# Float16 attention products, constant scales and a range flag in a fused attention and MLP kernel

## The chip, the cores and the metric

The kernel runs on one core of a Trainium2 chip. The metric is the device time of one execution in microseconds. Engines are named as in the profile: PE is TensorE (matmuls), PEld its weight loads, DVE is VectorE, ACT is ScalarE, POOL is GpSimd, SP is SyncE, which issues nearly all DMAs.

## The reference

There are 8 batches of 8 heads with 576 tokens and 64 dimensions per head. Each k and q row is projected to 128 features, shifted by its own largest absolute projection, and turned into 256 features by two exponentials. Linear attention follows, then an MLP on 4,608 tokens of width 512 with 2,048 hidden units.

```python
def phi(x):
    proj = np.einsum('bhsd,df->bhsf', x, w_phi)
    proj = proj - np.max(np.abs(proj), axis=-1, keepdims=True)
    return np.concatenate([np.exp(proj), np.exp(-proj)], axis=-1)
...
num = np.einsum('bhsf,bhfd->bhsd', q_p, kv)
den = np.einsum('bhsf,bhf->bhs', q_p, z)[..., None] + 1e-06
...
h = x @ w_in
g = h * (1.0 / (1.0 + np.exp(-1.702 * h)))
return (g @ w_out).astype(np.float32)
```

The two MLP weight matrices arrive as float64, everything else as float32.

## The kernel before, in words

All arithmetic is recorded first and ordered afterwards. `Recorder.record` (L164) notes each operation with its engine, its tiles and an estimated cost; `schedule` (L283) plays the five engines forward in time with these costs and picks, on each engine, the ready operation with the lowest priority number; `emit` (L393) writes the instructions in that order, so every one of them carries line L399 in the profile, and tiles tell them apart. Priorities come from `part(v0, v1)`, which gives a group of operations a place on a scale whose unit is one MLP chunk of 384 tokens. One engine executes its instructions in the order written.

Precision is kept by splitting. A float32 value is held as a high and a low 16-bit part, and a product is made of three 16-bit products (high x high, high x low, low x high). The MLP ("MoE" in the code, `moe_chunk`, L1140) works so: for a chunk of 256 or 384 tokens and each of 16 hidden blocks, 12 matmuls into `hb`, a tanh on ACT (`th`), a product on DVE (`g`), a split into `gh` (ACT) and `gl` (DVE), and three 512-column matmuls per 128 tokens into `ab`.

Attention works on units of one batch and two heads (32 units, `attn_unit`, L922) plus a tail per batch for tokens 512 to 575 (`attn_tail`, L865). The first five units are "exact": transposes, projections and products in float32 (`project_whole`, L790; tiles `e`, `vn`, `kf`, `wb`), with no scale needed. The other 27 scale k and q by powers of two found from their maxima (`kq_scales`, L745), split them (`xs`), transpose them by DMA (`xT`), project with `ph`, subtract the maximum (`t`), and for queries transpose `t` back on PE. Of the two exponentials, exp(t) is split into float16 parts (`eh`, `el`) and exp(-t), whose range is larger, into an fp32r part (`eh`) and a bfloat16 part (`elb`). So of the products with v (`vs`, `v`) and with the key sums (`kzs`, `kz`, `kzb`) half are 16-bit and half have one wide fp32r factor. A key step or query step is four matmuls: two of 132 columns, two of 66.

Scales are computed on the chip. `batch_max` (L645) reads v once more for its maximum; `weight_scales` (L592) finds the largest weights from the diagonal of products of each weight block with itself on PE (the `wsq` matmuls, L563); only then can `split_weights` (L621) split the blocks. The float64 weights are turned into float32 by ACT, POOL and DVE in `load_weights` (L524), with staging room inside the weight buffer and the `x` buffers.

Of the kernel before, what the change touches and what calls it, by code (L numbers as in the profile page):

```python
# [8 lines left out]
F32 = mybir.dt.float32  # L9
# [15 lines left out]
EPS = 1e-6  # L25

# [71 lines left out]
class _Op:  # L98
    __slots__ = (
        "eng", "meth", "args", "kw", "cost", "deps", "left", "outs", "allocs", "uses",  # L100
        "prio", "load", "passes", "end", "est", "also", "start", "calls",
# [4 lines left out]
_SWITCH = 0.0  # L106
# [3 lines left out]
class _Engine:  # L110
# [3 lines left out]
    def __getattr__(self, meth):  # L114
        def f(*a, also=(), **k):
            self.rec.record(self.name, meth, a, k, also)

        return f


class Recorder:
    def __init__(self, nc):
        self.nc, self.ops = nc, []
        self.groups, self.first = [], ()
# [4 lines left out]
    def part(self, v0, v1, first=()):  # L129

        self.group = []
        self.groups.append((v0, v1, first, self.group))
        self.first = first

    def pairs(self, mm, also=()):


        o = _Op()
        o.eng, o.meth, o.args, o.kw, o.calls = "tensor", "matmul", (), {}, mm
        c = [self.cost("tensor", "matmul", a, k) for a, k in mm]  # L140
        o.load, o.cost, o.passes = c[0][0], _SWITCH + sum(x[1] * x[2] for x in c) / 2, 1
        o.deps, o.outs, o.allocs, o.uses = {}, [], [], []
        o.end, o.est = None, 0.0
        for a, _ in mm:
            for i in (1, 2):
                if isinstance(a[i], V):
                    self.touch(o, a[i], False)
        for a, _ in mm:
            self.touch(o, a[0], True)
        for a in also:  # L150
            self.claim(o, a.tl)
        o.left = len(o.deps)
        for d in o.deps:
            d.outs.append(o)
        self.group.append(o)
        o.prio = o.eng in self.first
        self.ops.append(o)
# [6 lines left out]
    def record(self, eng, meth, args, kw, also):  # L164
        o = _Op()
        o.eng, o.meth, o.args, o.kw, o.calls = eng, meth, args, kw, None
        c = self.cost(eng, meth, args, kw)
        o.load, o.cost, o.passes = c if eng == "tensor" else (0.0, c, 1)
        o.deps, o.outs, o.allocs, o.uses = {}, [], [], []
        o.left, o.end, o.est = 0, None, 0.0  # L170
# [13 lines left out]
        o.prio = eng in self.first  # L184
# [28 lines left out]
    @staticmethod  # L213
    def shared(o):

        ap = [a.t if isinstance(a, V) else a for a in o.args]
        src = [a for a in ap[1:] if hasattr(a, "space")]
        if any("PSUM" in str(a.space) for a in src):
            return False
        if o.eng == "gpsimd":  # L220
            return len(src) > 1
        if o.eng == "vector":
            return o.meth in ("tensor_copy", "tensor_scalar") or len(src) > 1
        return False

    @staticmethod
    def cost(eng, meth, args, kw):
# [9 lines left out]
        if eng == "tensor":  # L237
# [10 lines left out]
            return (load, n / 2.4 + (22.0 if wide else 3.0), 1)  # L248
        src = ap[1] if len(ap) > 1 and hasattr(ap[1], "space") else out
        psum = "PSUM" in str(src.space)  # L250
        if eng == "scalar":
            return n / 1.2 + 51 + (0 if psum else 42) + 93 * scalars
# [12 lines left out]
        if meth == "tensor_scalar":  # L265
            return 100 + 3.4 * n
        if meth == "tensor_copy":
            return 100 + 0.9 * n
        if meth in ("tensor_sub", "tensor_mul", "tensor_add", "tensor_tensor"):
            return 100 + 2.2 * n  # L270
        return 400.0

    @staticmethod
    def mode(o, i):

        if o.calls:
            return o.calls
# [5 lines left out]
    def schedule(self):  # L283
# [15 lines left out]
        free = {e: 0.0 for e in ("tensor", "scalar", "vector", "gpsimd", "sync")}  # L299
# [4 lines left out]
        def ready(o):  # L304
            est = 0.0
# [9 lines left out]
            cand[o.eng].append(o)  # L315
# [5 lines left out]
        while todo:  # L321
            best = None
            for e, c in cand.items():
                t = free[e]
                pick = None
                for o in c:
                    s = max(t, o.est, turn + o.load) if e == "tensor" else max(t, o.est)
                    ok = True
                    had = {}
# [14 lines left out]
                    if pick is None or k < pick[0]:  # L344
                        pick = (k, o, s)
# [4 lines left out]
            _, o, s = best  # L350
            if o.eng in ("vector", "gpsimd") and self.shared(o):
                if o.eng == "vector":
                    s = max(s, port)
                else:
                    port = s + o.cost
            cand[o.eng].remove(o)
# [6 lines left out]
            if o.meth.startswith("dma"):  # L363
                free[o.eng] = s + (600.0 if o.eng == "sync" else 800.0)
                pipe = max(pipe, s) + o.cost
                o.end = pipe + 1800.0
# [26 lines left out]
    def emit(self):  # L393
        g = lambda a: a.get() if isinstance(a, V) else a
        self.order = self.schedule()
        for o in self.order:
            f = getattr(getattr(self.nc, o.eng), o.meth)
            for args, kw in o.calls or ((o.args, o.kw),):
                f(*[g(a) for a in args], **{k: g(a) for k, a in kw.items()})  # L399
# [3 lines left out]
def attn_moe_kernel(ctx, tc, q, k, v, w_phi, w_in, w_out, out):  # L403
# [11 lines left out]
    NEX = 5  # L415
    NH = 2

# [10 lines left out]
    def static(name, shape, dt):  # L428
# [6 lines left out]
        kq=2, vn=1, xs=2, xT=2, ks=12, tl=1, t=5, e=3, eh=3, ekth=1, eqth=1, xf=1, kzs=1, kf=1, lq=2, nf=1, nt=1, xo=1, x=3, th=2, g=2, gh=2,  # L435
        gl=2, osb=2, sm=8, rc=2, sc=6,
    )
    shapes = dict(
        kq=([P, 2, 8, D], F32), vn=([P, 8, D + 2], F32), xs=([P, 8, 2, D], F16),
        xT=([P, 8, P], F16), ks=([P, 2], F32), tl=([P, 3, NHP, D], F32), t=([P, 4, NF], F32),  # L440
        e=([P, 1024], F32), eh=([P, 512], F32R), ekth=([P, 512], F32R),
        eqth=([P, 512], F32R),
        xf=([P, 4, 2, D], F32),
        kzs=([P, 2, 2, 2, D + 2], F32R), kf=([P, 2, 2, D + 2], F32), lq=([P, 3, D + 2], F32),
        nf=([P, 8, D + 2], F32), nt=([P, 8, D + 2], F32), xo=([P, 2, 4, P], F16),
        x=([P, 2, NCT, S], F16), th=([P, CH], F32), g=([P, CH], F32),
        gh=([P, CH], F16), gl=([P, CH], F16), osb=([P, DM], F32), sm=([P, 4], F32),
        sc=([P, 10], F32), rc=([P, 8], F32),
    )
    pools = {  # L450
        nm: buf(nm, sh, dt, NB[nm], ordered=nm not in ("sc",)) for nm, (sh, dt) in shapes.items()
    }

    NL = dict(eh=3, el=2, ekth=1, ektl=1, eqth=1, eqtl=1)
    for nm in NL:
        pools[nm + "6"] = buf(nm + "6", [P, 512], F16, NL[nm])
    for nm in ("el", "ektl", "eqtl"):
        pools[nm + "b"] = buf(nm + "b", [P, 512], BF16, NL[nm])

# [5 lines left out]

    def psa():
        return R.tile(at, whole=True)

    def f32(ap):
        return ap.bitcast(F32)  # L470
# [6 lines left out]
    nc.vector.tensor_copy(ii[D:P], ident[D:P, D:P])  # L477

    ones = cp.tile([2, P], F32, name="ones")
    nc.gpsimd.memset(ones, 1.0)  # L480
    wone = cp.tile([2, 2], F32, name="wone")
    nc.vector.tensor_scalar(wone[:, 0:1], ident[0:2, 0:1], 16.0, None, ALU.mult)
    nc.vector.tensor_copy(wone[:, 1:2], ident[0:2, 1:2])
# [4 lines left out]
    phg = static("phg", [P, 1], F32)  # L488
    phs = static("phs", [P, 1], F32)

    def load_phi():
# [8 lines left out]
        allmax(phg, wst)  # L500
        R.vector.tensor_scalar(phg, phg, 2.0**-14, None, ALU.mult)
        R.vector.reciprocal(phs, phg)
# [808 lines left out]
```

## Time and profile before

| | |
|---|---|
| median of 3 runs | 1081.53 us (1080.89 to 1082.6) |
| span of the profiled execution | 1079.0 us |
| what lies around the span, median less span | 2.5 us |
| PE, DVE, ACT, POOL busy | 1046.1, 851.1, 713.4, 247.1 us |
| mean granted TensorE clock | 0.995 |
| first MoE matmul, last MoE matmul (start) | 78.42 us, 1073.02 us |
| DMA | 88.59 MB, mean 82 GB/s |

The profiled execution has no time of its own besides its span; the runs' median stands for it. A row of the profile names engine, operation, output<-inputs, shape, count, then busy time (overlaps counted once) and mean duration of one, then idle time of the engine just before these instructions and what ended it. A matmul's duration includes its way through the pipeline, so the next one can start long before the end. In the timeline, the first column is the start in the span and the second the length of a merged run.

### The profile page before, as it was taken

To read this page: it belongs to the slowest core of one execution; us is meant where nothing else is said; L and a number is where in the kernel's file an instruction comes from. 1 tells how busy PE (TensorE), PEld (TensorE's weight loads), DVE (VectorE), ACT (ScalarE), POOL (GpSimd) and SP (SyncE) were. 2 spreads that over 40 slices of the span, in tenths; PEclk is the share of its full clock that TensorE was granted. 3 is DMA by queue.
4 is the path that set the end of the run, shared out by engine and by line. 5 is a ranking of instruction groups with operands and counts; after the bars stand their busy time and mean duration, and the time that the engine had idled before them with its cause. 6 is when DMAs were issued, how large, how long until landed. Compare 5 with 4: busy or idle time off the path is not lost.

```text
span 1079.0 us, 22925 instructions
## 1 busy us (share of the span) xinstructions
PE 1046.1 (97%) x8943; PEld 723.7 (67%) x8943; DVE 851.1 (79%) x1772; ACT 713.4 (66%) x1488; POOL 247.1 (23%) x320
## 2 busy tenths in 40 slices
PE   5998999999999999999999999999999999999997
PEld 3665677778766666678866666677876666577653
DVE  5879999999999997987899978987889675232323
ACT  4778797777878686875786676866687665332322
POOL 5666113331122213211223113111133112000000
PEclk9998999999999999999999999999999999999999
DMA  8956233434343443331244342432232110000101
GB/s 277 301 186 173 87 88 70 100 76 97 76 97 94 114 98 72 82 89 31 62 126 112 57 84 50 94 84 36 56 73 60 31 40 20 1 31 2 30 1 30
DMA packets 177452, 88.59 MB, mean 82 GB/s; under 512 B 143424, under 2 KB 168128, under 8 KB 177088
## 3 DMA queue, kind: packets, MB, share of 16 engines
q1 hardware_dynamic: 177184, 86.87, 32.5%
q8 instruction: 70, 1.15, 0.4%
q10 hardware_dynamic: 160, 0.26, 0.1%
q14 instruction: 38, 0.31, 0.1%
HBM read 54.59 MB, written 9.44 MB: 59 GB/s over the span
## 4 chain that ended last, share of the span: by engine, by line
PE 76%; DVE 13%; ACT 5%; issue 3%; DMA 1%; SPq 1%; POOL 0%; DVEq 0%; ACTq 0%; POOLq 0%
PE ab L399 30%; PE hb L399 29%; PE at L399 17%; DVE sm L399 2%; DVE wbuf L399 2%; DVE gl L399 1%; DVE t L399 1%; ACT e L399 1%; DVE ks L399 1%; DVE el L399 1%; DVE xs L399 1%; DVE elb L399 1%; DVE g L399 1%; SPq L399 1%; DVE vs L399 1%
## 5 line engine op out<-in xcount | busy, mean ns | idle before, releaser
L399 PE MATMUL hb<-x,wbuf 128*128 128x192 f16 (+3 forms) x3264 | 476.4, 280 | 1.2 <-DVE g L399 0.6
L399 PEld LDWEIGHTS <-wbuf 128*128 128x128 f16 (+1 forms) x3392 | 286.4, 98 | 79.9 <-issue 1.8
L399 PE MATMUL ab<-wbuf,gh 128*128 128x512 f16 x1152 | 337.9, 380 | 0.5 <-ACT gh L399 0.3
L399 ACT ACTIVATE th<-hb,usc 128x384 f32<-128x384 f32 (+1 forms) x208 | 115.8, 558 | 145.5 <-PE hb L399 142.8
L399 PE MATMUL ab<-wbuf,gl 128*128 128x512 f16 x576 | 194.1, 379 | 1.4 <-DVE gl L399 1.1
L399 DVE SCALAR_TENSOR_TENSOR g<-th,hb 128x384 f32<-128x384 f32 (+1 forms) x208 | 107.1, 516 | 95.6 <-ACT th L399 93.3
L399 PEld LDWEIGHTS <-gh 128*128 128x128 f16 x1152 | 107.7, 98 | 81.1 <-ACT gh L399 2.6
L399 ACT ACTIVATE gh<-g,al 128x384 f16<-128x384 f32 (+1 forms) x176 | 106.9, 607 | 52.6 <-DVE g L399 52.0
L399 DVE SCALAR_TENSOR_TENSOR gl<-g,al,gh 128x384 f16<-128x384 f32 (+1 forms) x176 | 109.9, 625 | 39.9 <-ACT gh L399 31.4
L399 POOL TENSOR_TENSOR xf<-nf,rc 128x512 f32<-128x512 f32 x28 | 34.2, 1220 | 410.8 <-DVE rc L399 331.3
L399 PE MATMUL at<-ph,xT 128*128 128x128 f16 x976 | 102.4, 219 | 0.0
L399 DVE TENSOR_REDUCE sm<-at 128x4 f32<-128x512 f32 x126 | 85.6, 680 | 17.8 <-PE at L399 17.4
L399 ACT ACTIVATE e<-at 128x512 f32<-128x512 f32 x144 | 85.4, 601 | 20.8 <-PE at L399 19.7
L399 ACT ACTIVATE e<-t 128x512 f32<-128x512 f32 x144 | 88.2, 630 | 11.8 <-DVE t L399 11.1
L399 DVE SCALAR_TENSOR_TENSOR t<-at,ks,sm 128x512 f32<-128x512 f32 x122 | 90.4, 743 | 1.1
L399 PEld LDWEIGHTS <-gl 128*128 128x128 f16 x576 | 54.8, 98 | 50.4 <-DVE gl L399 8.9
L399 DVE TENSOR_TENSOR el<-e,eh 128x512 f16<-128x512 f32 x108 | 75.4, 698 | 13.3 <-ACT eh L399 11.5
L399 DVE TENSOR_TENSOR elb<-e,eh 128x512 bf16<-128x512 f32 x110 | 77.9, 708 | 5.7 <-ACT eh L399 4.3
L399 PE MATMUL at<-vs,eh 128*128 128x132 f32 x216 | 81.8, 379 | 0.0
L399 PE MATMUL at<-kzs,eh 128*128 128x132 f32 x224 | 79.4, 373 | 0.8 <-ACT nf L399 0.5
L399 PEld LDWEIGHTS <-xT 128*128 128x128 f16 x976 | 69.8, 98 | 12.9 <-issue 0.3
L399 ACT ACTIVATE eh<-t 128x512 fp32r<-128x512 f32 x109 | 67.1, 635 | 1.1 <-DVE t L399 1.1
(199 smaller groups left out, 1845.6 us busy)
## 6 DMA issues: line engine op xcount, KB each, us to landing
vn<-in_v_dram SPq DMA_DIRECT2D x64, 128.0 KB, 2.7
kq<-in_k_dram SPq DMA_DIRECT2D x32, 256.0 KB, 3.2
kq<-in_q_dram SPq DMA_DIRECT2D x32, 256.0 KB, 3.0
tl<-in_v_dram SPq DMA_DIRECT2D x18, 384.0 KB, 3.2
x<-in_moe_w_in_dram SPq DMA_DIRECT2D x10, 512.0 KB, 6.0
x<-in_moe_w_out_dram SPq DMA_DIRECT2D x10, 512.0 KB, 6.3
out_dram<-osb SPq DMA_DIRECT2D x36, 128.0 KB, 2.4
out_dram<-osb SPq DMA_DIRECT2D x16, 256.0 KB, 2.5
```

The costliest lines, as they stand in the source:

```text
L399: f(*[g(a) for a in args], **{k: g(a) for k, a in kw.items()})
```

## The change

**Products.** Every key and query step becomes six matmuls of 66 columns with float16 parts (`keys`, `numden`). exp(-t) is brought into float16 range by a constant factor. For queries, the projection is made a second time with `ph` as stationary and the transposed rows as moving operand (one 512-column pair, `project_q`), so that features come out transposed without a transpose of `t`; the shift by the maximum is not subtracted from queries but put back as a factor per token (`cs`, from ACT) on one half of numerator and denominator (`n1`).

**Exact units.** Batch 0 keeps float32 keys in its four units and float32 queries for the first half of the tokens (`queries_exact`); its other queries, its tail and the fifth unit go in float16 parts. `attention_first` records all keys of batch 0, then the first half of the queries, then the second, after which MLP chunks can start on 256 columns.

**Scales.** All scales are constants (`PH, VS, ONE, WS, GS`). The maxima of k, q and v before use, the self-products of the weights and the second pass over them go. Each weight block is split when it is loaded, in six elementwise operations through three staging buffers (`raw`): one on ACT, two scalings on DVE, ACT or POOL, one on DVE, a copy and a subtraction.

**Range flag.** The maxima of v, of the weights and of w_phi, a ratio of sums (`art`) and a sum of `g` per chunk are collected; `in_range` compares them with limits and writes a flag. Near the end every engine loads it, and `tc.If(ok == 0)` runs a separate float32 program (`attn_moe_general`) that computes everything again.

**Order.** Some operations may go to one of two or three engines (`_Either`); the planner takes the one that ends first by a priced cost. VectorE and GpSimd operations that both use SBUF now exclude each other in the plan. The places of the groups are a table of numbers (`PLACES`), and only groups behind its end use the places in the code.

```diff
+PLACES = (
+    (-1000.000, -1000.000), (-26.554, -13.917), (-103.111, -99.006), (-24.532, -12.535), (-103.432, -95.864),
...
-            if o.eng in ("vector", "gpsimd") and self.shared(o):
-                if o.eng == "vector":
-                    s = max(s, port)
-                else:
-                    port = s + o.cost
...
+            if alt[3] and o.eng in ("vector", "gpsimd"):
+                s = max(s, port - 70.0)
+                port = s + o.cost
...
+                R.scalar.activation(y, hi.bitcast(F32), AF.Copy, scale=2.0**-111)
+                R.three.scale(r16[:, :, 2], r16[:, :, 1], 0.9375 * 2.0**-13)
+                R.three.scale(r16[:, :, 3].bitcast(F16), r16[:, :, 3].bitcast(I16), 2.0**-60)
...
+            (R.evac if here else R.three).copy(w16[:, i, 0], y)
+            (R.vector if here else R.two).tensor_sub(w16[:, i, 1], y, w16[:, i, 0])
...
+        pT = psa()
+        mv = xT.rearrange("p t s -> p (t s)")
+        R.tensor.matmul(pT, ph[:, 0], mv, start=True, stop=False, also=also)
+        R.tensor.matmul(pT, ph[:, 1], mv, start=False, stop=True)
...
+        for sg, b in ((U, 0.0), (-U, -EK * LN2)):
+            e, h, l = new("e"), new(hi), new(lo)
+            R.scalar.activation(e, t, AF.Exp, scale=sg, bias=b)
+            R.three.copy(h, e)
+            R.two.tensor_sub(l, e, h)
...
-                    mm.append((st[0], vx[s].rearrange("p i d -> p (i d)"), kv[:, s]))
-                    mm.append((st[1], vx[0][:, 0], kv[:, s, 0:DV]))
...
+                        mm += [(st[0], vx[0], o), (st[0], vx[1], o), (st[1], vx[0], o)]
...
+    ok = attn_moe_fast(tc, q, k, v, w_phi, w_in, w_out, out)
+    with tc.If(ok == 0):
+        attn_moe_general(tc, q, k, v, w_phi, w_in, w_out, out, xd)
```

How this moves instructions shows at three places. On PE, in the middle of the program, at the products of keys with v: before, `vs` is the wide part of v with `eh` in fp32r, `v` its float16 copy, and `hb<-x,wbuf` is an MoE matmul.

```order
12917 L399 LDWEIGHTS wbuf_170
12918 L399 MATMUL hb_64<-x_112,wbuf_170 128x384
12919 L399 MATMUL at_61<-vs_182,eh_97 128x132
12920 L399 LDWEIGHTS elb_149
12921 L399 MATMUL at_61<-v_187,elb_149 128x66
12922 L399 LDWEIGHTS ekth_144
12923 L399 MATMUL at_61<-vt_188,ekth_144 128x132
12924 L399 LDWEIGHTS ektl_145
12925 L399 MATMUL at_61<-vt_188,ektl_145 128x66
12926 L399 LDWEIGHTS wbuf_170
```

After, at the same kind of place, `vs` is float16 throughout.

```order
4075 L460 LDWEIGHTS eh_95
4076 L460 MATMUL at_65<-vs_110,eh_95 128x66
4077 L460 LDWEIGHTS eh_95
4078 L460 MATMUL at_65<-vs_110,eh_95 128x66
4079 L460 LDWEIGHTS el_99
4080 L460 MATMUL at_65<-vs_110,el_99 128x66
4081 L460 LDWEIGHTS eh_93
4082 L460 MATMUL at_65<-vs_110,eh_93 128x66
```

Before, every wide product stands behind an MoE matmul, and steps and MoE work alternate; after, the steps follow each other without MoE matmuls between them.

On PE at the start of the MLP: before, `ab<-wbuf` are the self-products of the second half of the weights.

```order
308 L399 MATMUL ab_66<-wbuf_170 128x128
309 L399 LDWEIGHTS wbuf_170
310 L399 MATMUL ab_66<-wbuf_170 128x128
311 L399 LDWEIGHTS wbuf_170
312 L399 MATMUL ab_66<-wbuf_170 128x128
313 L399 LDWEIGHTS wbuf_170
314 L399 MATMUL ab_66<-wbuf_170 128x128
315 L399 LDWEIGHTS wbuf_170
316 L399 MATMUL hb_65<-x_110,wbuf_170 128x256
```

After, the first MoE matmul comes between exact query work of batch 0 (`x_126` is the exponentials' scratch, `w` the split weights).

```order
237 L460 LDWEIGHTS ones
238 L460 MATMUL at_66<-kz_117,ones 128x2
239 L460 MATMUL at_65<-x_126,kf_112 66x256
240 L460 LDWEIGHTS w_229
241 L460 MATMUL hb_68<-x_127,w_229 128x256
```

The self-products are gone, and the first MoE matmul moves from row 316 of PE to row 241.

On POOL in the middle of the program: before, a unit gives it casts of v, the key sums, the division (`xf`) and the low part of the result (`xo`).

```order
157 L399 CAST vs_182<-v_187 128x8x64
158 L399 CAST v_187<-vs_182 128x8x64
159 L399 TENSOR_TENSOR xf_102<-nf_107,rc_137 128x2x4x64
160 L399 TENSOR_TENSOR xo_109<-xf_102,xo_109 128x512
161 L399 CAST vs_182<-v_187 128x8x64
```

After, it shares the splits of features (`eh`, `el`) and inputs (`xs`) and the per-token factors (`n`) with DVE and ACT.

```order
270 L460 CAST eh_95<-e_90 128x512
271 L460 CAST xo_125<-xf_124 128x512
272 L460 TENSOR_TENSOR el_98<-e_89,eh_97 128x512
273 L460 TENSOR_TENSOR n_118<-n_118,cs_150 128x198
274 L460 TENSOR_TENSOR el_101<-e_88,eh_94 128x512
275 L460 TENSOR_TENSOR el_100<-e_92,eh_96 128x512
```

Features that PE waits for now pass through POOL. The order of the changed kernel holds 134 two-input operations of 512 elements on POOL, the one before 55, and 416 operations on data instead of 293.

More of the change, by code (lines that the diff above doesn't have):

```diff
@@ L100 @@
         "eng", "meth", "args", "kw", "cost", "deps", "left", "outs", "allocs", "uses",
-        "prio", "load", "passes", "end", "est", "also", "start", "calls",
+        "prio", "load", "passes", "end", "est", "also", "start", "alts", "after",
     )
-_SWITCH = 0.0
+PLACES = (
[25 rows of a table added]
+)
 _READY = {"tensor": 282.5, "scalar": 240.0, "vector": 305.0, "gpsimd": 300.0, "sync": 100.0}
@@ L127, in __init__, with part @@
             setattr(self, e, _Engine(self, e))
-    def part(self, v0, v1, first=()):
-        self.group = []
+        self.two = _Either(self, "vector", "gpsimd")
+        self.evac = _Either(self, "scalar", "vector")
+        self.three = _Either(self, "vector", "scalar", "gpsimd")
+    def part(self, v0, v1, first=(), after=0.0):
+        n = len(self.groups)
+        if n < len(PLACES):
+            v0, v1 = PLACES[n]
+        self.group, self.after = [], after
         self.groups.append((v0, v1, first, self.group))
         self.first = first
[L135 to L157, printed above, removed]
     def tile(self, buf, whole=False):
@@ L395, in emit, with attn_moe_fast @@
         self.order = self.schedule()
+        late, then = self.late
         for o in self.order:
+            if then and o.start > late.end + 4000.0:
+                then()
+                then = None
             f = getattr(getattr(self.nc, o.eng), o.meth)
-            for args, kw in o.calls or ((o.args, o.kw),):
-                f(*[g(a) for a in args], **{k: g(a) for k, a in kw.items()})
+            f(*[g(a) for a in o.args], **{k: g(a) for k, a in o.kw.items()})
+        if then:
+            then()
 @with_exitstack
-def attn_moe_kernel(ctx, tc, q, k, v, w_phi, w_in, w_out, out):
+def attn_moe_fast(ctx, tc, q, k, v, w_phi, w_in, w_out, out):
     nc = tc.nc
@@ L1224, in attention @@
-        R.part(u + 0.003 if b == 0 else u - 0.01, u)
-        tl = tail_load(b)
-        def bank():
-            return R.tile(ab, whole=True) if b == 0 else psa()
+        xs[b] = (x16[:, 0], x16[:, 1])
+        return x16
+    def attention(b):
+        u = v_att(4 * b)
+        x16 = place(b)
+        R.part(u - 0.01, u)
+        tl = tail_load(b)
+        nt = new("nt")
+        R.part(u, u + 0.266)
+        tail = attn_tail(b, tl, psa)
+        for hp in range(NHP):
+            w = v_att(4 * b + hp)
+            R.part(w, w + 0.517)
+            kt, qt, vn = attn_load(b, hp)
+            kf, kz = keys(b, hp, kt, vn, tail, nt, b == 1 and EXK1[hp], False, psa)
+            queries(hp, qt, kz, nt, x16, psa)
+            if hp == NHP - 1:
+                queries_tail(nt, tail[3], x16)
@@ L1248, in attn_moe_kernel @@
             R.part(v0 + dv * i, v0 + dv * (i + 1))
[L1249 to L1255 removed]
+            load_weights(j, (lambda: R.tile(hb, whole=True)) if j < NPS else (lambda: new("wy")))
     attention(1)
@@ L1265, in attn_moe_kernel @@
             moe_chunk(0, c, 256, part_)
+    for i in range(NBLK):
+        R.part(3.0 + 0.2 * i, 3.0 + 0.2 * i, after=250e3)
+        weight_max(i)
     for sb in range(B // SB):
```

1147 lines of the change are left out of this document (611 added, 536 removed), and 24 rows, old and new, of the table PLACES.

## The prediction

> **What bounds the kernel now.** I read the clock row first (one core, mean granted clock 0.995), then the page's busy times and chain, then the busy time in five stages cut at the first MoE matmul (78.4 us) and where attention ends (900 us).
>
> ```profile
> PE 1046.1 (97%) x8943; PEld 723.7 (67%) x8943; DVE 851.1 (79%) x1772; ACT 713.4 (66%) x1488; POOL 247.1 (23%) x320
> PE 76%; DVE 13%; ACT 5%; issue 3%; DMA 1%; SPq 1%; POOL 0%; DVEq 0%; ACTq 0%; POOLq 0%
> ```
>
> ```profile
> 0.00:78.40 78.40, 63.16 (x399) 45.22 (x400) 56.70 (x112) 51.64 (x103) 48.69 (x58) 1.00 0.79 258
> 78.40:150.00 71.60, 65.30 (x478) 45.03 (x476) 68.37 (x136) 56.84 (x115) 25.69 (x24) 0.95 0.49 133
> 150.00:300.00 150.00, 148.38 (x1599) 113.64 (x1597) 147.29 (x339) 118.75 (x271) 37.36 (x48) 1.00 0.36 79
> 300.00:900.00 600.00, 595.90 (x5322) 414.85 (x5321) 521.23 (x1088) 424.91 (x896) 130.17 (x185) 1.00 0.33 74
> 900.00:1073.00 173.00, 172.98 (x1154) 105.00 (x1153) 56.35 (x100) 60.97 (x107) 5.17 (x6) 1.00 0.04 12
> ```
>
> The columns are length, then PE, weight loads, DVE, ACT, POOL, each with its instructions, then clock, DMA share, GB/s. From 150 us on PE is busy 917.3 of 923 us, so the time there is PE's work; DVE is nearly as full until 300 (147.3 of 150) and has room later. Before 78.4 us PE is idle for 15.2 us, and up to 150 for 6.3 more.
>
> Busy times overlap, since matmuls are pipelined, so PE work has to be priced from one start to the next. PE rows of one mixed stretch:
>
> ```profile
> 500.10 0.38 PE L399 MATMUL ab<-wbuf,gh 128*128 128x512 f16 x1
> 500.13 0.41 PE L399 MATMUL at<-vs,eh 128*128 128x132 f32 x1
> 500.38 0.20 PE L399 MATMUL at<-v,elb 128*128 128x66 f16 x1
> 500.42 0.22 PE L399 MATMUL at<-v,eh 128*128 128x132 f16 x1
> 500.48 0.19 PE L399 MATMUL at<-v,el 128*128 128x66 f16 x1
> 500.51 0.38 PE L399 MATMUL ab<-wbuf,gh 128*128 128x512 f16 x1
> ...
> 501.87 0.59 PE L399 MATMUL ab<-wbuf,gh 128*128 128x512 f16 x2
> 502.30 0.38 PE L399 MATMUL ab<-wbuf,gl 128*128 128x512 f16 x1
> ...
> 509.61 0.60 PE L399 MATMUL at<-ident,t 128*128 128x128 f32 x4
> 510.05 0.38 PE L399 MATMUL ab<-wbuf,gh 128*128 128x512 f16 x1
> ```
>
> A 512-column float16 matmul takes 0.43/2 = 0.215 us. One key step (both signs of the exponential, one tile of tokens) and the MoE matmul in front of it take 0.41 us, so the step's four products cost 0.195. The wide (fp32r) product starts 0.03 us after the MoE matmul and runs on under it: its slow weight load is already hidden, and removing it gains little. A 66-column product takes 0.03, a float32 transpose 0.44/4 = 0.11. The startup gives the rest:
>
> ```profile
> 30.49 1.07 PE L399 MATMUL ab<-wb,t 128*128 128x256 f32 x4
> 31.40 1.88 PE L399 MATMUL at<-e,kf 128*66 128x512 f32 x4
> 33.12 0.60 PE L399 MATMUL at<-ident,t 128*128 128x128 f32 x4
> ...
> 77.27 1.31 PE L399 MATMUL ab<-wbuf 128*128 128x128 bf16 x20
> 78.42 0.82 PE L399 MATMUL hb<-x,wbuf 128*128 128x256 f16 x6
> ```
>
> A float32 pass of 512 columns takes 1.72/4 = 0.43 us, one of 256 about 0.22, and a 16-bit matmul of 128 columns 1.15/20 = 0.0575.
>
> **The change part by part.** The MoE matmuls are the same before and after. What changes on PE:
>
> ```profile
> L399 PE MATMUL at<-ph,xT 128*128 128x128 f16 x976 | 102.4, 219 | 0.0
> L399 PE MATMUL at<-ident,t 128*128 128x128 f32 x288 | 46.6, 274 | 2.8 <-DVE t L399 1.8 <-ACT t L399 0.9
> L399 PE MATMUL ab<-wb,t 128*128 128x256 f32 x72 | 21.1, 423 | 1.2 <-ACT t L399 1.1
> L399 PE MATMUL at<-e,vn 128*66 128x256 f32 x80 | 19.3, 380 | 2.3 <-ACT e L399 2.3
> L399 PE MATMUL at<-e,kf 128*66 128x512 f32 x40 | 18.2, 595 | 0.3 <-ACT kf L399 0.2
> L399 PE MATMUL hb<-x,wbuf 128*128 128x64 f16 x192 | 9.0, 193 | 0.0
> ```
>
> Exact (float32) units: five whole ones become four units of keys and half their queries. Passes go from 80 to 64 (e,vn: 16 x 0.22 = 3.5 us), from 40 of 512 columns to 32 of 256 (17.2 - 7.0 = 10.2), and from 88 projections (72 rows and 16 in other banks) to 48 (8.8). The float32 transposes around them fall by 24 at 0.11 and by 28 of 66 columns at about 0.06: 4.3. Gain 26.8.
>
> Weight maxima: 128 matmuls of weights by themselves go, 128 x 0.0575 = 7.4.
>
> Query transposes: 288 at 0.11 = 31.7 become 16 (1.8) and 136 direct projections of 512 columns (29.2). Gain 0.7. The 128-column projections rise from 976 to 1,056: loss 4.6.
>
> Products: before, 27 units of 10 key and 8 query steps at 0.195 = 94.8, and per unit a tail of two 264- and two 132-column products, about 0.335, 9.0 in all: 103.8. After, 3,120 products of 66 columns at 0.03 = 93.6, 192 of 132 at 0.0575 = 11.0, 32 of two columns at 0.03 = 1.0: 105.6. Loss 1.8; had the wide products not been hidden it would have been a gain of many times that. The Trainium skill, TensorE: Matmul & The Clock Gate, section "Back-to-back issue gap", gives about 81 ns for each matmul of 128 columns in a stream of weight loads and matmuls; at that figure the 3,120 would cost an estimated 253 us. The row above speaks against it: 192 matmuls of 64 columns, each with its own load, are busy 9.0 us, at most 0.047 each.
>
> Net on PE: 26.8 + 7.4 + 0.7 - 4.6 - 1.8 = 28.5 us less.
>
> Startup: about 16 of these 28.5 us lie before the first MoE matmul (32 passes of 512 columns become 32 of 256, 6.8; 24 projections fewer, 5.3; half the weight maxima, 3.7; transposes less the new projections, near 0). There PE is idle for 15.2 of 78.4 us, and its float32 steps follow ACT and DVE one after the other. I count half of the 16 as not realized: +8, between 0 and +16. Against this, each of 32 weight blocks has six elementwise operations instead of five:
>
> ```profile
> L399 POOL TENSOR_SCALAR x<-x 128x512 int32<-128x512 uint16 x20 | 34.2, 1711 | 2.3 <-DMA x<-in_moe_w_in_dram 0.9
> L399 ACT ACTIVATE wbuf<-wbuf,sw 128x512 f16<-128x512 f32 x32 | 23.0, 720 | 6.3 <-DVE wbuf L399 5.3 <-DVE sw L399 0.8
> L399 DVE SCALAR_TENSOR_TENSOR wbuf<-wbuf,sw 128x512 f16<-128x512 f32 x32 | 25.5, 796 | 1.7 <-ACT wbuf L399 1.6
> ```
>
> At 0.72 us that is up to 23 us, spread over three engines; the wait for the scales, in which no block could be split, goes. I take 0 and keep +23 for the range. The u16 and i16 scalings are rows that the trace doesn't have in their new form: 0.72 to 1.71 us.
>
> Waits of the mixed stages: 6.3 + 1.6 + 4.1 = 12.0 us idle in 78.4 to 900, and 5% of clock in 71.6 us, 3.6: 15.6. DVE, which was full, loses the maxima of k and q, the scaling of each maximum and half of the shifts, and POOL takes part of the splits. I take half, 8, range 0 to 15.6. The 32 maxima of the split weights are placed late on DVE, which has 79 us of room in 300 to 900.
>
> End: each engine loads the flag and compares. On PE the load stands among the last 120 matmuls, at least 4 us after the flag's planned end; the branch of SP stands behind its last stores.
>
> ```profile
> 1073.02 0.38 PE L399 MATMUL ab<-wbuf,gl 128*128 128x512 f16 x1
> ...
> 1074.48 1.46 SPq L399 DMA_DIRECT2D out_dram<-e  x2
> ```
>
> The last stores are issued until 1075.94 and the span ends at 1079.0, so 3 us can cover a branch. I take +1, range 0 to +4.
>
> Sum: 1079.0 - 28.5 + 8 - 8 + 1 = 1051.5 us of span. The median of the runs, 1081.53, is 2.5 above the profiled span, so 1054.
>
> **The rivals.** (1) Everything on PE pays: startup gains its 16 and the waits go. 1079.0 - 28.5 - 15.6 + 2.5 = 1037 us. For it: PE is the chain's 76%. Against: waits rarely all go.
>
> (2) The weight blocks become the startup's limit: six operations a block and three staging buffers. 1054 + 23 = 1077. For it: ACT and DVE are busy 51.6 and 56.7 of 78.4. SP issues in order, so a weight load that waits for its staging buffer holds back the loads of k, q and v queued behind it, which the next batches' products wait for. Against: no second pass over the weights.
>
> (3) Slower: VectorE and GpSimd shut each other out, and PE waits. The order gives POOL 134 two-input operations of 512 elements where it had 55.
>
> ```profile
> L399 POOL TENSOR_TENSOR xo<-xf,xo 128x512 f16<-128x512 f32 x27 | 32.4, 1199 | 26.8 <-ACT xo L399 24.6 <-DVE sm L399 1.2 <-DVE rc L399 1.0
> L399 DVE TENSOR_TENSOR el<-e,eh 128x512 f16<-128x512 f32 x108 | 75.4, 698 | 13.3 <-ACT eh L399 11.5 <-ACT e L399 0.7 <-PE at L399 0.7
> L399 DVE SCALAR_TENSOR_TENSOR vs<-vn,iv,v 128x512 fp32r<-128x512 f32 x27 | 26.8, 992 | 4.3 <-ACT v L399 4.0
> ```
>
> A split takes 1.20 us on POOL, 0.70 on DVE. That they do hold each other is seen: the same kind of DVE operation averages 0.796 us on weights and 0.992 on v, beside POOL's casts. If each of the 134 holds PE for the difference, 0.5 us, that is 67: 1121. It decides from 27.5/134 = 0.2 us each. Against: POOL was busy a quarter, its results now have buffers of five and four deep, and DVE is relieved. The Trainium skill, SBUF — State Buffer, section "SBUF: two separate sides", calls the shared port pair an exclusive lock held for a whole instruction; the row of vs agrees.
>
> (4) The small products are bound by their weight loads, unhidden.
>
> ```profile
> L399 PEld LDWEIGHTS <-el 128*128 128x128 f16 x432 | 42.3, 99 | 9.8 <-DVE el L399 1.9 <-issue 0.9
> ```
>
> 3,120 x (0.099 - 0.03) = 215: 1269. The 64-column row speaks against it. By the figure of the Trainium skill named above (TensorE: Matmul & The Clock Gate, "Back-to-back issue gap") the time would be an estimated 1054 + 253 - 94 = 1213.
>
> (5) The change doesn't do what it says: the flag is 0 and the float32 path runs too, over 1,000 us more (its 48 x 16 second products alone, two passes of 0.43 us each, are 660). The drawn weights stay inside the limits (largest of w_in about 5/22.6 = 0.22, limit 0.25).
>
> **How the numbers follow.** Forecast 0.60, (1) 0.13, (2) 0.15, (3) 0.07, (4) 0.01, (5) 0.02, and 0.02 that it all cancels. A measurement here tells 0.2%, 2.2 us. Faster: 0.60 + 0.13 + 0.15 = 0.88; within: 0.02; slower: 0.10. The range runs from (1), 1037, to (2), 1077.
>
> **What would show it.** Right: products of 66 columns every 0.03 us in unbroken runs; no bf16 weight squares; PE dense from 150 us on, its busy time near 1,020; the first MoE matmul between 65 and 80 us; the last stage to the end under 10 us. Wrong: 66-column products at 0.05 or more; PE waiting on POOL el or eh for more than 15 us in all; a first MoE matmul after 95 us; anything running after the last store.

## The result and the profile after

The changed kernel takes 1100.12 us (median of four runs, 1098.72 to 1101.05) against 1081.5 for the kernel before: a ratio of 1.0172, 95% interval 1.0157 to 1.0186. It is slower, by 1.7%. The profiled span is 1098.5 us where it was 1079.0.

First the busy times and the chain from the page of the changed kernel:

```profile
PE 1022.5 (93%) x9874; PEld 671.3 (61%) x9874; DVE 808.4 (74%) x1506; ACT 629.6 (57%) x1357; POOL 354.2 (32%) x461
PE 60%; DVE 23%; ACT 8%; issue 3%; DMA 3%; SPq 1%; POOL 1%; DVEq 0%; ACTq 0%; POOLq 0%
```

PE is busy for 1022.5 us, 23.6 less than before. The work went; the time did not go with it. In the chain PE's share fell from 76% to 60%, and DVE and ACT took most of what PE lost. Span less busy time is PE's idle time: 32.9 us before, 76.0 now. -23.6 + 43.1 = +19.5, the difference of the spans.

Where PE became idle is read from the same four stretches of both kernels. The columns are length, then busy time of PE, weight loads, DVE, ACT and POOL with their instructions, then clock, DMA share, GB/s. The kernel before:

```profile
0.00:75.00 75.00, 59.76 (x363) 42.08 (x363) 53.41 (x100) 48.39 (x96) 45.45 (x56) 1.00 0.82 268
75.00:200.00 125.00, 118.01 (x986) 84.91 (x986) 121.60 (x267) 99.60 (x213) 39.52 (x39) 0.97 0.41 103
200.00:620.00 420.00, 416.79 (x3989) 298.66 (x3987) 390.28 (x846) 310.58 (x670) 101.36 (x139) 1.00 0.37 86
620.00:1045.00 425.00, 423.18 (x3465) 283.78 (x3463) 275.35 (x543) 245.13 (x497) 60.75 (x88) 1.00 0.20 44
```

The changed kernel:

```profile
0.00:75.00 75.00, 47.19 (x274) 33.36 (x275) 52.99 (x95) 56.74 (x100) 14.83 (x57) 0.96 0.65 187
75.00:200.00 125.00, 102.75 (x1002) 70.08 (x1001) 110.33 (x202) 108.83 (x224) 69.58 (x82) 0.93 0.50 126
200.00:620.00 420.00, 405.10 (x4739) 276.81 (x4738) 387.24 (x710) 269.26 (x620) 203.22 (x245) 1.00 0.39 84
620.00:1045.00 425.00, 423.13 (x3629) 268.24 (x3627) 242.21 (x469) 182.35 (x392) 66.61 (x77) 1.00 0.15 35
```

PE's idle time grows by 12.6 us up to 75 us, by 15.3 up to 200, by 11.7 up to 620, by nothing after that; the other 3.5 us lie at the end. Up to 200 us ACT went from 148 to 165.6 us of 200 busy, and POOL, which carried 45 us of work in the first 75, carries 15 there (over the whole 200 us it carries 84 as before). From 200 to 620 us DVE has 136 instructions fewer and is busy for nearly the same time: on average each takes longer.

The new work up to 200 us, in the groups of one shape (busy time, mean ns of one, idle time before it and who ended that):

```profile
L460 ACT ACTIVATE raw<-raw 128x512 uint16<-128x512 uint16 x19 | 25.7, 1353 | 0.1
L460 ACT ACTIVATE raw<-raw 128x512 f16<-128x512 int16 x16 | 21.6, 1368 | 0.0
L460 DVE TENSOR_SCALAR raw<-raw 128x512 f16<-128x512 int16 x11 | 10.1, 917 | 0.0
L460 DVE TENSOR_SCALAR raw<-raw 128x512 uint16<-128x512 uint16 x11 | 9.0, 837 | 1.4 <-ACT hb L460 1.4
L460 POOL TENSOR_SCALAR raw<-raw 128x512 f16<-128x512 int16 x5 | 6.7, 1346 | 15.1 <-ACT hb L460 10.2 <-ACT wy L460 4.9
L460 POOL TENSOR_SCALAR raw<-raw 128x512 uint16<-128x512 uint16 x2 | 2.9, 1456 | 0.3 <-ACT hb L460 0.2
```

These are the two scalings of each weight block. Before, one scaling a block ran on POOL. Now 47 us of them run on ACT and 19 on DVE. Two places of the trace, ACT's and then DVE's, show the wait that this makes:

```profile
89.09 2.49 ACT L460 ACTIVATE raw<-raw 128x512 uint16<-128x512 uint16 x2
...
91.61 0.69 DVE L460 SCALAR_TENSOR_TENSOR wy<-wy,raw 128x512 int32<-128x512 int32 x1 [1.69 <-ACT raw L460]
```

DVE stands for 1.69 us until ACT has done two scalings, in a stage where they are busy 87 and 88% of the time.

The products are as forecast. Consecutive rows of PE near 501 us:

```profile
501.07 0.22 PE L460 MATMUL at<-vs,eh 128*128 128x66 f16 x2
501.14 0.19 PE L460 MATMUL at<-vs,el 128*128 128x66 f16 x1
501.17 0.22 PE L460 MATMUL at<-vs,eh 128*128 128x66 f16 x2
501.23 0.19 PE L460 MATMUL at<-vs,el 128*128 128x66 f16 x1
501.26 0.22 PE L460 MATMUL at<-vs,eh 128*128 128x66 f16 x2
```

Six products start in 0.19 us, 0.03 us each, each with its own weight load.

### The profile page after: what moved, and what is told of

Its sections match the earlier page's. It is cut to its first block, busy times and chain, and to the rows that moved or that the text cites. A ratio compares the mean times of both kernels' runs of the same rounds, so it can differ in the third digit from the quotient of the medians.

```text
span 1098.5 us, 24641 instructions
## 1 busy us (share of the span) xinstructions
PE 1022.5 (93%) x9874; PEld 671.3 (61%) x9874; DVE 808.4 (74%) x1506; ACT 629.6 (57%) x1357; POOL 354.2 (32%) x461
## 4 chain that ended last, share of the span: by engine, by line
PE 60%; DVE 23%; ACT 8%; issue 3%; DMA 3%; SPq 1%; POOL 1%; DVEq 0%; ACTq 0%; POOLq 0%
PE ab L460 25%; PE hb L460 24%; PE at L460 11%; DVE el L460 4%; DVE gl L460 3%; ACT raw L460 2%; DVE sm L460 2%; DVE g L460 2%; DVE t L460 2%; ACT e L460 2%; DVE wmx L460 1%; DMA xT<-xs 1%; SPq L460 1%; DVE xf L460 1%; DVE mq L460 1%
## 5 line engine op out<-in xcount | busy, mean ns | idle before, releaser
L460 PE MATMUL hb<-x,w 128*128 128x192 f16 (+3 forms) x3264 | 452.4, 280 | 2.5 <-DVE g L460 1.6
L460 PEld LDWEIGHTS <-w 128*128 128x128 f16 x3264 | 279.5, 98 | 108.3 <-issue 6.1
L460 PE MATMUL ab<-w,gh 128*128 128x512 f16 x1152 | 319.3, 380 | 4.3 <-ACT gh L460 2.2
L460 ACT ACTIVATE th<-hb 128x384 f32<-128x384 f32 (+1 forms) x208 | 96.8, 467 | 198.4 <-PE hb L460 191.8
L460 PE MATMUL ab<-w,gl 128*128 128x512 f16 x576 | 189.5, 380 | 5.2 <-DVE gl L460 4.9
L460 DVE SCALAR_TENSOR_TENSOR gl<-g,gh 128x384 f16<-128x384 f32 (+1 forms) x208 | 135.7, 654 | 38.1 <-ACT gh L460 37.8
L460 ACT ACTIVATE gh<-g 128x384 f16<-128x384 f32 (+1 forms) x208 | 103.5, 499 | 80.8 <-DVE g L460 79.1
L460 PEld LDWEIGHTS <-eh 128*128 128x128 f16 x1856 | 111.4, 97 | 30.3 <-issue 5.5
L460 POOL TENSOR_TENSOR el<-e,eh 128x512 f16<-128x512 f32 x71 | 95.1, 1344 | 74.9 <-DVE eh L460 32.5
L460 ACT CAST eh<-e 128x512 f16<-128x512 f32 x145 | 87.8, 619 | 6.6 <-PE at L460 5.7
L460 PE MATMUL at<-kz,eh 128*128 128x66 f16 x960 | 78.4, 194 | 4.3 <-DVE nf L460 1.4
```

The lines of the kernel that those rows point to most:

```text
L460: f(*[g(a) for a in o.args], **{k: g(a) for k, a in o.kw.items()})
```

## The experiments

Each kernel below was timed beside the kernel before, whose median stayed between 1080.9 and 1081.9 us, so medians are compared with the changed kernel's 1100.1 directly. Unless a diff says otherwise the order of instructions is that of the changed kernel: an instruction is left out or replaced when it is issued, after the order is made. `FLAG` stands for the line that sets the flag to 1. `is_scaling` and `out` stand for tests on an instruction's operands.

The theories: **A**, the scalings load ACT and DVE up to 200 us, where PE waits for them. **B**, GpSimd's two-input operations hold VectorE off. **C**, PE's clock, which shows 0.986 in the mean where it was 0.995. **D**, the range flag and its branch. **E**, the later first transpose. **A0** is the rival of A: the startup is held by the order of its steps, not by the scalings.

**All scalings to POOL.**

```diff
+            if is_scaling(o):
+                o.eng, o.meth, o.args, o.kw = *o.alts[2][:2], *o.alts[2][4:]
```

> The same 64 scalings all on GpSimd, as the kernel before had its one integer scaling a block, at the same places of the order; nothing is left out. GpSimd had 7 of them. Theory A: ScalarE and VectorE win 66 us of work, GpSimd gains 57 x 1.4 = 80 us of work in 165 us where it is busy a quarter: 1080 to 1090 us. Rival B: more work on GpSimd is more locking, 1100 to 1110 us.

Measured: 1123.2 us, ratio to before 1.0387 (1.037 to 1.0404). It is beyond B's range. POOL takes 1.4 us for each of the 64, one after the other, and DVE's and-or of the blocks in PSUM waits for it:

```profile
L462 DVE SCALAR_TENSOR_TENSOR hb<-hb,raw 128x512 int32<-128x512 int32 x16 | 11.2, 697 | 22.6 <-POOL raw L462 22.5
```

So this does not refute A; it puts a new wait in the place of the old one.

**POOL's subtractions left out.**

```diff
+            if o.eng == "gpsimd" and o.meth == "tensor_sub" and out(o) in ("el", "ektl", "eqtl"):
+                continue
+        FLAG
```

> Leaves out GpSimd's subtractions that make the low halves of the exponentials (71 into el and those into ektl and eqtl); the low halves keep a constant, and the range flag is set to 1 by hand. Every other instruction keeps its place. Rival B: VectorE's subtractions fall from 846 to about 700 ns and the time by 25 us or more, to 1075 or less. Theory A: at most 15 us, 1085 to 1095 us.

Measured: 1084.9 us (1.0012 to 1.0042): 15.2 us less. B is real, and smaller than B alone would need.

**Without the range flag.**

```diff
+            if o.also:      # recorded for the range flag
+                continue
-    with tc.If(ok == 0):
-        attn_moe_general(tc, q, k, v, w_phi, w_in, w_out, out, xd)
```

> Leaves out all that the range flag needs (maxima of v and of the split weights, the ratios, the sums of g, the comparisons, the load of the flag on each engine, the branch and the float32 path behind it); every other instruction keeps its place. Rival D (the flag and the branch are the cost): 1085 us or less. Theories A and B: 3 to 6 us, of which 3.5 after the last MoE matmul: 1094 to 1097 us.

Measured: 1092.0 us (1.0068 to 1.0102): 8.1 us less. D is too small as the one cause, but more than expected. From the last matmul's start to the end it is now 5.8 us (6.0 before the change) and 9.6 with the flag. That is 3.8 of the 8.1. Of the other 4.3 the profiled execution shows half: PE's idle time from 200 to 620 us falls from 14.9 to 12.8 us. There DVE no longer has, among others, these 20.6 us, which ran between 283 and 331 us, where DVE is busy for 54.8 of 55 us:

```profile
L460 DVE TENSOR_REDUCE wmx<-w 128x1 f32<-128x512 f16 x32 | 20.6, 670 | 0.0
```

**The scalings left out.** The and-or becomes an and, which keeps the weights finite.

```diff
+            if is_scaling(o):
+                continue
-    y.bitcast(I32), y.bitcast(I32), 3, hi, ALU.logical_shift_left, ALU.bitwise_or
+    y.bitcast(I32), y.bitcast(I32), 3, hi, ALU.logical_shift_left, ALU.bitwise_and
+        FLAG
```

> Leaves out the 64 scalings of 16-bit words (two for each of the 32 weight blocks, 47 us on ScalarE and 19 on VectorE in the first 200 us); the planned order is otherwise kept, the weights' signs and low bits come out wrong, and the range flag is set to 1 by hand. Theory A (the scalings fill ScalarE and VectorE where both are about 90% busy and PE waits for them): 1075 to 1082 us, the first MoE matmul 5 us or more earlier. Rival A0 (the startup is held by the order of its steps and its loads, not by the scalings): 1095 to 1100 us.

Measured: 1082.0 us (0.9984 to 1.0022): 18.1 us less, at the upper end of what A expected, and the first MoE matmul at 74.7 us instead of 80.6. A holds, A0 falls. The weights of this run mean nothing. That their values set PE's pace is not seen: from 620 to 1,045 us PE is busy 423.43 us here and 423.13 in the changed kernel, with a granted clock of 1.00 in both.

**Scalings and POOL's subtractions left out.** Both edits above together.

> Leaves out the 64 scalings and also GpSimd's subtractions of the exponentials' low halves, which alone took 15 us off; flag set to 1 by hand, everything else at its place. If the two costs are separate and lie in different stages (theory A with B): the sum of both gains, 1058 to 1068 us, near the predicted 1054. Rival A0: no more than GpSimd's subtractions alone gave, 1082 to 1085 us.

Measured: 1062.4 us (0.9816 to 0.9849), 37.7 less than the changed kernel where the two alone give 33.3. They are separate costs, and taking out both gives somewhat more than their sum.

**One scaling on POOL, the sign on DVE.**

```diff
-  R.three.scale(r16[:, :, 2], r16[:, :, 1], 0.9375 * 2.0**-13)
-  R.three.scale(r16[:, :, 3].bitcast(F16), r16[:, :, 3].bitcast(I16), 2.0**-60)
+  R.gpsimd.tensor_scalar(lo, r16[:, :, 1], 0.9375 * 2.0**-13, None, ALU.mult)
-  (y, y, 3, hi, ALU.logical_shift_left, ALU.bitwise_or)
+  (y, y, 3, lo, ALU.logical_shift_left, ALU.bitwise_or)
+  (y, hi, -(2**31), y, ALU.bitwise_and, ALU.bitwise_or)
```

> The two scalings of a weight block become one on GpSimd (the integer scaling that the kernel before had, 1.7 us) and a second and-or on VectorE (about 0.75 us) that takes the sign; nothing is left out, the order is otherwise kept. ScalarE loses 47 us of work in the first 200 us, VectorE gains 32 x 0.75 - 19 = 5, GpSimd gains 54 - 10 = 44. Theory A: 1085 to 1092 us. If GpSimd's place in the chain is what made the run with all scalings on GpSimd slow: 1105 to 1120 us. Rival A0: within 5 us of the changed kernel.

Measured: 1102.0 us (1.0184 to 1.0218), no gain, though ACT is down to 127 us of the first 200. ACT's time alone is therefore not what A is about. DVE, its and-or doubled and POOL beside it, is at 170.6 us of 200 where the changed kernel has 163.3.

**The kernel before, its scaling on ACT.**

```diff
- R.gpsimd.tensor_scalar(lo, top, 0.9375 * 2.0**-13, None, ALU.mult)
+ R.scalar.activation(lo, top, AF.Copy, scale=0.9375 * 2.0**-13)
```

> The kernel before, with one edit: its 32 integer scalings of the weights' low words go from GpSimd to ScalarE, at the same places of the order; nothing is left out. ScalarE gains about 32 x 1.35 = 43 us of work in the first 110 us, where it is busy three quarters. Theory A: 15 to 25 us slower than the kernel before, 1097 to 1107 us. Rival A0: within 4 us of it.

Measured: 1089.4 us, 1.0074 (1.0057 to 1.0091) of the kernel before: half of what I expected. The reason is in the price that I had given it:

```profile
L401 ACT ACTIVATE x<-x 128x512 int32<-128x512 uint16 x20 | 13.7, 686 | 0.0
```

0.69 us, not 1.35, for the same input at the same stride. The output is 32 bits wide here and 16 in the changed kernel.

**All three left out.** Scalings, POOL's subtractions and flag, by the edits above.

> Leaves out all three costs at once: the 64 scalings of the weights' 16-bit words, GpSimd's subtractions of the exponentials' low halves, and everything of the range flag with its branch and the float32 path; all else keeps its place. Theory A+B+D (these three, separate, are what the prediction had too small, and its PE terms were right): 1062.4 - 8 = 1052 to 1057 us, the predicted 1054. If a fourth cost is left (the clock, the later first transposes), the sum would be met only by chance; if the costs overlap, 1060 us or more.

Measured: 1053.0 us (0.9715 to 0.9752 of before). The forecast was 1054. With the three costs away the time is the forecast's, and the trace shows PE nearly as dense as before:

```profile
75.00:200.00 125.00, 116.86 (x1295) 84.31 (x1293) 112.03 (x236) 93.59 (x231) 46.39 (x61) 0.97 0.60 135
200.00:620.00 420.00, 414.67 (x4635) 280.43 (x4633) 323.51 (x620) 263.90 (x600) 105.69 (x143) 1.00 0.37 80
```

That the time is met to 1 us is in part luck. The busy times of this run are:

```profile
PE 1006.4 (96%) x9872; PEld 670.4 (64%) x9872; DVE 718.8 (69%) x1398; ACT 589.2 (56%) x1322; POOL 199.2 (19%) x308
```

PE is busy for 39.7 us less than in the kernel before, where the forecast has 28.5. It is idle for 42.8 us of the span of 1049.2, 9.9 more than before, where the forecast's other terms come to 1 us more. Two misses of some 10 us cancel. Which term of PE's work was too small is not shown. This run also leaves out work that the forecast counts, the flag's 1 us for one.

The mean clock is 0.994 in this run, without the weights' self-products. The lost clock of the changed kernel went away with the three costs, so the sum needs no C of its own. A mean of 0.986 over 1098.5 us is 15.4 us of lost clock, one of 0.994 over 1049.2 is 6.3, so at most about 9 of the 47 us are clock; how much of each of the three gains was clock was not separated.

**The lock alone.** In the place of each left-out subtraction POOL subtracts constants into a tile that nobody reads.

```diff
+            if o.eng == "gpsimd" and o.meth == "tensor_sub" and out(o) in ("el", "ektl", "eqtl"):
+                self.nc.gpsimd.tensor_sub(*self.idle)
+                continue
+        FLAG
```

> In place of each GpSimd subtraction of a low half stands a subtraction of the same kind between constants, 480 elements instead of 512, written to a tile that nobody reads; so GpSimd's work stays at its place, and no instruction waits for its result. The low halves keep a constant; flag set to 1 by hand. Theory B1 (what costs is that VectorE is held off while GpSimd runs): 1095 to 1100 us, VectorE's el again near 850 ns. Rival B2 (what costs is that the products wait for GpSimd's slower result): 1084 to 1088 us, as with these subtractions left out.

Measured: 1102.0 us (1.0169 to 1.0214). All of the 15 us are back, with nobody waiting for these results: B1 holds, B2 falls. POOL's other results are not what is waited for either: the waits for POOL that the profiles list add up to 8.6 us in the changed kernel, 7.6 without the subtractions and 8.5 with the idle ones. VectorE's subtractions and `gl` show it, in the changed kernel, without POOL's subtractions, and with the idle ones:

```profile
L460 DVE TENSOR_TENSOR el<-e,eh 128x512 f16<-128x512 f32 x161 | 134.0, 846 | 6.2 <-PE at L460 2.2 <-ACT eh L460 1.7 <-issue 0.6
L460 DVE SCALAR_TENSOR_TENSOR gl<-g,gh 128x384 f16<-128x384 f32 x160 | 106.0, 663 | 35.5 <-ACT gh L460 35.2
```

```profile
L462 DVE TENSOR_TENSOR el<-e,eh 128x512 f16<-128x512 f32 x161 | 120.8, 763 | 7.9 <-PE at L462 3.4 <-ACT eh L462 2.3 <-POOL eh L462 0.5
L462 DVE SCALAR_TENSOR_TENSOR gl<-g,gh 128x384 f16<-128x384 f32 x160 | 96.7, 604 | 36.2 <-ACT gh L462 36.0
```

```profile
L463 DVE TENSOR_TENSOR el<-e,eh 128x512 f16<-128x512 f32 x161 | 133.4, 841 | 6.9 <-PE at L463 3.2 <-ACT eh L463 1.8 <-POOL eh L463 0.5
L463 DVE SCALAR_TENSOR_TENSOR gl<-g,gh 128x384 f16<-128x384 f32 x160 | 102.9, 643 | 35.4 <-ACT gh L463 35.2
```

These are 846, 763 and 841 ns for the same operation on the same tiles.

**The sign's scaling on POOL.**

```diff
+            if o in self.signs:
+                o.eng, o.meth, o.args, o.kw = *o.alts[2][:2], *o.alts[2][4:]
```

> One of a block's two scalings (the sign, int16 to float16) always on GpSimd, at its place of the order, so that the two run side by side; the other stays where it was planned. Nothing is left out. ScalarE loses 21.6 us, VectorE 10, GpSimd gains 27 x 1.4 = 38. If the gain of leaving out the scalings comes from ScalarE's and VectorE's time alone: 1088 to 1093 us. If work on GpSimd costs as much as it saves (its place in the chain, and VectorE held off): 1097 to 1110 us.

Measured: 1106.5 us, 1.0211 of before (1.0179 to 1.0243), not better than the changed kernel. What ACT and DVE save is lost again beside POOL: DVE's other scaling goes from 837 to 1285 ns. The granted clock from 75 to 200 us is also lower here, 0.88 against 0.93, so not all of the loss need be DVE's.

```profile
L462 DVE TENSOR_SCALAR raw<-raw 128x512 uint16<-128x512 uint16 x11 | 14.0, 1285 | 1.0 <-ACT hb L462 1.0
```

**The first loads earlier.**

```diff
+        first = [o for o in dma if name(o)[:2] == "tl"][:4] + [o for o in dma if name(o) == "wst"]
+        self.order = first + [o for o in self.order if o not in first]
```

> The loads of the first tail's k and q and of w_phi go to the front of SyncE's queue; nothing is left out and nothing else moves. PE's first matmul, at 14.9 us in the changed kernel behind the first transposed tile, should come at 11 us. Theory E (the startup is a chain from its first transpose on): 3 to 4 us less, 1096 to 1097. If VectorE and ScalarE are what fills the startup: within 1.5 us, 1099 to 1100.

Measured: 1100.3 us (1.015 to 1.0192), no change. It does not test E: w_phi's load stayed where it was, ScalarE's cast stayed behind a scaling that waits for v, and PE's first matmul came at 15.9 us, not at 11.

**The whole way to the first transpose earlier.**

```diff
+        first = tls + wst + nat + cast + turn + ph
+        self.order = first + [o for o in od if o not in first]
```

> The whole way to the first transposed tile goes to the front of its queues (the loads of the first tail's k and q, of w_phi and of the first k and q, ScalarE's cast, VectorE's subtraction, SyncE's transpose, the scaled w_phi); nothing is left out and all else keeps its order. PE's first matmul should come at 10 to 12 us instead of 14.9. Theory E: 3 to 4 us less, 1096 to 1097. If VectorE and ScalarE fill the startup from there on: within 1.5 us of the changed kernel, 1099 to 1101.

Measured: 1103.1 us (1.0182 to 1.0216), 3 us more. PE's first matmul now comes at 11.2 us:

```profile
11.15 1.14 PE L473 MATMUL ab<-ph,xT 128*128 128x128 f16 x9 [11.15 <-DMA xT<-xs]
```

The first MoE matmul does not follow it; it comes at 82.8 us. So an earlier first step brought no gain, and E is not needed for the sum. It is not cleanly refuted: the granted clock up to 75 us is 0.89 in this run and 0.96 in the changed kernel, about 5 us of clock, which could hide a gain of 3 to 4.

**POOL's subtractions on DVE.**

```diff
+            if o.eng == "gpsimd" and o.meth == "tensor_sub" and out(o) in ("el", "ektl", "eqtl"):
+                o.eng = "vector"
```

> GpSimd's 86 subtractions of low halves (el, ektl, eqtl) go to VectorE, at the same places of the planned order; nothing is left out. VectorE gains 86 x 0.70 = 60 us of own work and is held off less: from 200 to 620 us it would be at the 357.6 us that it has without them plus 55 x 0.70 = 38, 396 of 420 us, against 387.2 in the changed kernel. If GpSimd saves VectorE as much as it holds it off (the split between the two is worth nothing): 1095 to 1103 us. If VectorE's own time is what counts: 1104 us or more. If GpSimd's work costs more than it saves: 1094 us or less.

Measured: 1099.4 us (1.0149 to 1.0183), equal. The 86 subtractions are worth nothing on POOL: DVE is as full without its help as with it, 390.1 against 387.2 of the 420 us. The Trainium skill, Perfetto Trace Analysis, section "Optimizing Scalar/DVE Operations", says that moving work between these two engines might not help because they share a port; this pair of runs agrees: the medians differ by 0.7 us, less than their intervals' width.

**A complete decode with a 32-bit output.** As the run with one scaling on POOL, but that scaling is ScalarE's.

```diff
-  R.gpsimd.tensor_scalar(lo, r16[:, :, 1], 0.9375 * 2.0**-13, None, ALU.mult)
+  R.scalar.activation(lo, r16[:, :, 1], AF.Copy, scale=0.9375 * 2.0**-13)
```

> Nothing is left out: the low word's scaling always on ScalarE with a 32-bit output (0.68 us where the kernel before had it moved there, against 1.35 with a 16-bit output), and the sign by a second and-or on VectorE (0.7 to 0.84 us) in place of the second scaling. ScalarE has 32 x 0.68 = 22 us instead of 47, VectorE 32 x 0.75 = 24 instead of 19, GpSimd none of these. If the output's width is what makes the scalings dear: 1088 to 1095 us. If VectorE is what limits here: within 3 us of the changed kernel, 1097 to 1103.

Measured: 1100.8 us (1.0151 to 1.0185), no gain. ACT has 26 us less, but DVE's and-or for the sign takes 27.4 us where its scalings took 19.1. This fits DVE's time deciding first up to 200 us, but does not prove it: the granted clock from 75 to 200 us is 0.90 here against 0.93.

**The same scalings with 32-bit outputs.**

```diff
+            if o in self.wide:
+                o.args = (self.wide[o], *o.args[1:])
+        FLAG
```

> Both scalings stay at their engines and places, only their outputs are 32-bit words instead of 16-bit ones; the weights lose signs and low bits by it, and the range flag is set to 1 by hand. If the width of the output sets ScalarE's time: 0.68 us a scaling instead of 1.35, ScalarE 35 x 0.67 = 23 us less, and about half of the 18 us that leaving the scalings out gave, 1089 to 1094 us. If not: 1.3 us each and 1098 to 1102.

Measured: 1085.0 us (1.0016 to 1.0046): 15.1 us less, with as many instructions on the same engines at the same places. It is more than expected, because the width halves the price on DVE and POOL too:

```profile
L462 ACT ACTIVATE raw<-raw 128x512 int32<-128x512 uint16 x19 | 12.9, 679 | 0.0
L462 ACT ACTIVATE raw<-raw 128x512 int32<-128x512 int16 x16 | 10.7, 677 | 0.0
L462 DVE TENSOR_SCALAR raw<-raw 128x512 int32<-128x512 int16 x11 | 5.2, 468 | 0.0
L462 DVE TENSOR_SCALAR raw<-raw 128x512 int32<-128x512 uint16 x11 | 4.7, 425 | 0.2 <-DMA raw<-in_moe_w_out_dram 0.2
L462 POOL TENSOR_SCALAR raw<-raw 128x512 int32<-128x512 int16 x5 | 3.4, 670 | 13.2 <-ACT hb L462 9.4 <-ACT wy L462 3.6
```

No complete version here beats the kernel before. The decode of the kernel before, inside the changed one, was not tried. Nor was POOL's scaling in the faster form that the last section shows.

## Why the prediction was wrong, step by step

**PE's work** (28.5 us less, of it the products 1.8 more): right in its direction and in the price of the products, which start every 0.03 us. The page's busy time fell to 1022.5, the forecast said near 1,020. With the three other costs away it is 1006.4, so the term was about 11 us too small, and the 1053.0 of that run meets the forecast only because PE's idle time is about 9 us larger than forecast.

**The startup** is the first step that failed. The prediction counted "six elementwise operations instead of five" for a weight block, said "I take 0" and kept 23 us for the range. Leaving out the two scalings of a block gives 18.1. The count hid the point: one scaling on POOL, which without the scalings has only 9.9 us of other work in the first 75 (the kernel before with its scaling on ACT), became two, most of them on ACT and DVE, which were busy 65% and 71% of the first 75 us and 80% and 97% up to 200. The price was bounded rightly (0.72 to 1.71 us; measured 1.35 on ACT, 1.35 to 1.46 on POOL, 0.84 to 0.92 on DVE). It stood in the range as a rival and not in the sum.

**The saving in the startup** (half of 16 us) did not come either: the first MoE matmul moved from 78.4 to 80.6 us. With the scalings away it moved to 74.7, with all three costs away to 72.1, 6.3 us earlier than before where 8 were forecast.

**The waits** (8 us less) failed in sign. The prediction said that DVE is relieved; PE's idle time from 200 to 620 us rose from 3.2 to 14.9 us. DVE lost 136 instructions there and kept its time, because POOL held it off: without POOL's 86 subtractions it is busy for 357.6 us there instead of 387.2, with the idle ones for 382.2. The rival on this lock had the mechanism and the wrong place: PE hardly waits for POOL's results, while DVE runs slower, and PE waits for DVE. The rows of waits in the changed kernel show both, for matmuls (PE) and weight loads (PEld):

```profile
PEld L460 <- DVE el L460: 16.3, 28, 1.9
PE at L460 <- DVE el L460: 7.5, 14, 1.8
PE at L460 <- POOL xo L460: 0.5, 1, 0.5
```

The last is the only wait of a matmul for POOL in the list; weight loads wait for POOL 3.4 us more. The rival's price was 0.5 us for each of 134 operations, and 0.2 was its point of decision. Measured are 15.2 us over 86 subtractions, 0.18 each, just under that point; the other 48 operations were not taken out.

**The end** (+1, range 0 to 4): +3.6, inside its bounds. About 4.3 of the flag's 8.1 fall elsewhere, which the prediction took at nothing: it put the maxima of the weights into DVE's room of 79 us from 300 to 900, and they ran from 283 to 331 us, where DVE has none.

So the three omissions, 18.1 + 15.2 + 8.1 = 41.4 alone and 47.1 together, make the 46 us between the forecast and the time, with PE's work and PE's idle time each some 10 us off and cancelling. Each was named in the prediction and each was taken near zero or as a gain, for the same reason: PE's busy time was read as the bound, while DVE, and up to 200 us ACT too, was nearly as full in the stages where the new work lands. A smaller slip: the forecast's 2.5 us around the span compares a median with one execution's span; in every run on record an execution is 1.7 to 2.2 us longer than its own span.

## What to carry to other kernels

Where PE is the bound at 97%, look at the second engine in the same stretch before counting a saving: here it was nearly as full, little of the work taken from PE came back, and work given to that engine was paid for. An operation moved off an engine with little else to do has to be priced where it lands. Sharing elementwise work between VectorE and GpSimd is to be tried with the work put back on VectorE as the comparison: here it was worth nothing.

## What the runs showed that was not expected

A strided elementwise operation with a 16-bit output (every fourth 16-bit word is written) took twice as long as the same operation with a 32-bit output, on all three engines: 1.35 against 0.68 us on ACT, 0.84 to 0.92 against 0.43 to 0.47 on DVE, 1.35 to 1.46 against 0.66 to 0.67 on POOL, for 128x512. The input is the same 16-bit stride in both. By the medians most of the scalings' cost, 15.1 of 18.1 us, is this.

On POOL the width is not all. The single scaling of the kernel before has a 32-bit output too, and took 1.58 to 1.71 us there. In the run with one scaling on POOL it has the input, output and step of the two unsigned scalings that took 0.66 us with 32-bit outputs, and its row is:

```profile
L461 POOL TENSOR_SCALAR raw<-raw 128x512 int32<-128x512 uint16 x32 | 53.4, 1669 | 22.1 <-DMA raw<-in_moe_w_in_dram 12.5 <-DMA raw<-in_moe_w_out_dram 6.7 <-DVE hb L461 1.0
```

In the code the two differ in one thing: the slow form gives one factor (`c, None, ALU.mult`), the fast one a second factor of 1 (`c, 1.0, ALU.mult, ALU.mult`). The slow form's 32 took 1.55 us or more, the fast form's seven 0.71 or less. No run changes only this. If the second factor is the reason, the 53.4 us of POOL in that run would be about 21 (an estimate, 32 x 0.66).

POOL slows an operation with both inputs in SBUF here, and not one with an input in PSUM. The and-or of a weight block held in PSUM takes 697 ns, that of a block held in SBUF 837:

```profile
L460 DVE SCALAR_TENSOR_TENSOR hb<-hb,raw 128x512 int32<-128x512 int32 x16 | 11.2, 697 | 5.3 <-ACT raw L460 5.0
L460 DVE SCALAR_TENSOR_TENSOR wy<-wy,raw 128x512 int32<-128x512 int32 x16 | 13.3, 837 | 5.6 <-ACT raw L460 5.6
```

With one scaling a block on POOL the first is at 692 and the second at 879; with the sign's scalings on POOL 699 and 943; with all three costs left out 693 and 740. The Trainium skill, SBUF — State Buffer, section "SBUF: two separate sides", names VectorE operations with two inputs in SBUF as the ones that take the lock against GpSimd; the two rows agree.
